# A one-core attention decode kernel: start-up zeroing removed, second V load issued early, tail reordered

## The chip, the cores and the metric

One core of one Trainium2 chip. The metric is the device time of one execution in microseconds, median of several. Executions of the kernel before spread over some 2 us. The span that a profile shows is about 1.8 us shorter than the time (350.1 us and 351.93 us for the profiled execution of before).

A word on two readings that recur. The *timeline* and the *chain of waits* are views of the profile. The *landing* of a load is the time at which the last of its 16 semaphore increments arrived; the trace records it, and tables of landings below are taken from there. The engines have the profile's names: PE is the matmul engine (TensorE), DVE VectorE, ACT ScalarE, POOL GpSimd and SP SyncE, which issues the large loads. The *granted clock* (PEclk) is the share of PE's full clock that the profile records as granted; in the tables it is 1.00 or 0.50, or a mean of the two.

## The reference

A decode step for batch 2: attention of one query over a cache of 4096 keys for 32 heads, a small MLP, and a gate that mixes the two.

```python
# B = 2, Sq = 1, D = 512; H = 32 heads (Hkv = 32 too), Sk = 4096, Dh = 128; Dff = 1376
x = A_x
g = sigmoid((x * gate_w).sum(-1, keepdims=True))
q = x @ A_wq                                  # per head
p = softmax(q k^T * Dh ** -0.5)               # k_cache, v_cache: [B, H, Sk, Dh], bf16
a = (p v) @ A_wo
b = relu(x @ B_w1) @ B_w2
return g * a + (1 - g) * b
```

K and V are 67 MB each and are read once. All inputs together are 145.46 MB.

## The kernel before

Sixteen stages of four heads. In a stage a K tile of 4 MiB is multiplied on the DVE by the query, which has been broadcast over partitions (`mult`), the PE sums the products with an identity matrix (`red_mm`), the DVE finishes the sums, ACT takes the exponential, and the PE multiplies the probabilities with V (`pv`). K and V have two buffers each; every large load is issued by one queue, in order. At the end the heads' outputs are transposed into `OT_sb` and projected with `A_wo` (`wo_mm`), and the result is added (`wo_add`) in the PSUM tile of the MLP's second product (`mlp_o`).

```python
    load(SP, ring("wq"), ...); load(SP, ring("w1"), ...)
    load_k(0); load_k(1); load_v(0)
    ...
    issue(POOL, lambda e: e.memset(vt[1], 0.0), rd=[sel], wr=vb[1])   # the second V buffer
    ...
    # xb[b]: one column of x, broadcast; the queries' matmuls need it
    src = xT.ap[:, :, b : b + 1].to_broadcast([P, DC, TP])
    issue(DVE, ... e.tensor_copy(out=xb[b].ap, in_=src), rd=[xT], wr=[xb[b]])
    ...
    open_loop(NS // 2)          # on PE two stages are one trip of a hardware loop
    for s in range(NS):
        sums_mm(s - 1)
        mult(s, 0); evac(s - 2); expand(s - 1); sums_inv(s - 1)
        red_mm(s, 0); comb_mm(s - 2); mult(s, 1); unpack(s - 2)
        scores(s, 0); red_mm(s, 1); scores(s, 1); probs(s)
        pv(s - 1)               # for s = 0 on the zeroed buffer, result unused
        ...
        load_k(s + 2)           # waits for red_mm(s, 1): the buffer's last reader
        load_v(s + 1)           # waits for pv(s - 1)
        ...                     # at s = NS - 2 the last quarters of A_wo, and B_w2
    close_loop()

    s = NS - 1
    expand(s); evac(s - 1); sums_mm(s); comb_mm(s - 1); unpack(s - 1); sums_inv(s)
    for g in range(NG - 2):                     # half of the projection ...
        for h in range(2):
            wo_mm(g, h)
    pv(s, VC)                                   # ... ahead of the last P.V
    evac(s); comb_mm(s); unpack(s)
    for g in (NG - 2, NG - 1):
        for h in range(2):
            wo_mm(g, h)
    for n in range(len(W2CUTS)):
        if n == 2:
            wo_add()
        mlp_o(n)
    # cast to bf16, store
```

The softmax here doesn't subtract the row's maximum and nothing guards it: scores larger than these inputs give would overflow.

## Time and profile before

| | before |
|---|---|
| time, median of 5 | 352.83 us (351.62 to 353.13) |
| span of the profiled execution | 350.1 us |
| bytes moved | 145.46 MB |
| share of 16 DMA engines' span used by the load queue | 97.2% |
| PE, DVE busy | 60%, 61% |

The page of the kernel before; the two rows of forty entries are equal slices of the span (8.75 us each), the DMA row in tenths:

```profile
span 350.1 us, 2576 instructions
...
DMA  7999999999999999999999999999999999999990
GB/s 307 453 419 427 459 371 427 446 438 421 421 423 453 438 423 419 419 434 420 463 419 423 449 442 423 419 423 457 438 419 419 427 464 424 419 423 427 416 398 14
...
q1 hardware_dynamic: 6628, 145.46, 97.2%
```

DMA is full in every slice but the first and the last. Its rate dips below the usual 416 to 464 in the first slice, the sixth (371) and the last two. So the kernel is a stream of loads, and PE and DVE matter only where they hold the stream up, or where work is left after it.

The landings make this exact (issue and landing in us from the start of the span; "since" is the time since the landing before it):

```
load (KiB)            issue    landing   since
wq   (4096)            0.96     13.31
w1   (1376)            1.41     16.62    3.31
K 1  (4096)            1.88     26.35    9.73
K 2  (4096)            2.35     36.06    9.71
V 1  (4096)            2.92     46.99   10.92   <- 1.2 late
K 3  (4096)           43.93     56.70    9.71
V 2  (4096)           45.78     66.77   10.08   <- 0.4 late
...  every 4096 KiB load 9.71 to 9.74, except
K 15 (4096)          271.12    296.14   10.68   <- 1.0 late
...
w2, last part (128)  328.07    343.76    0.33
```

4 MiB in 9.71 us is 432 GB/s. Everything that lands "late" moves the whole rest of the stream, because the queue is in order (the loads land in the order of their issue) and full (97.2% of the span).

The head on the timeline (start us, duration us, engine, line, operation, output<-inputs, shapes, count; in brackets the idle time before and what ended it):

```profile
4.14 13.75 POOL L451 MEMSET vt<- 128x16384 bf16 x1
...
8.64 9.40 DVE L468 COPY xb<-xT 128x128 bf16<-128x128 bf16 x2
17.96 0.41 DVE L473 COPY gwb<-xT 128x512 bf16<-128x512 bf16 x1
...
29.55 8.72 DVE L594 TENSOR_TENSOR kt<-kt,qb 128x8192 bf16<-128x8192 bf16 x2
...
43.93 0.33 SPq L115 DMA_DIRECT2D kt<-in_A_k_cache_dram  x1
```

POOL fills the second V buffer for 13.75 us. Two small DVE copies beside it take 9.40 us and end 0.15 us after the fill, while a copy four times as large right after takes 0.41. The first K multiply starts 3.2 us after K 1 landed, and K 3 is issued at 43.93, when little is left in the queue.

The tail on the timeline:

```profile
334.12 3.18 PE L270 MATMUL mm<-wbig,OT_sb 128*2 128x512 bf16 x14
...
337.37 2.09 PE L270 MATMUL o<-vt,pt 128*32 128x512 bf16 x26
...
341.45 3.18 PE L270 MATMUL mm<-wbig,OT_sb 128*2 128x512 bf16 x14
...
344.69 1.25 PE L270 MATMUL a<-w,hT 128*2 128x256 bf16 x14
...
346.93 0.42 DVE L809 CAST res<-a 34x256 bf16<-34x256 f32 x1 [1.15 <-PE a L270]
```

The projection (`mm<-wbig,OT_sb`) runs at 0.2 us per matmul, half of it before the last P·V product (`o<-vt,pt`). The chain of waits confirms that the end is PE work (start us, duration us, what):

```profile
337.74 1.77 PE o L270 x23
...
341.52 3.44 PE mm L270 x16
...
346.93 0.42 DVE res L809
```

### The profile page before, as it was taken

The page shows a single profiled execution, that of the slowest core. Times are in us where ns is not written, and L with a number is a line of the kernel's source. Part 1 is how long each engine was busy: PE and PEld are TensorE (multiplying, and loading weights), DVE is VectorE, ACT ScalarE, POOL GpSimd, SP SyncE. Part 2 cuts the span into 40 slices and gives each one's busy share as a digit, 9 for nine tenths or more (in the row PEclk, how much of TensorE's full clock was granted, in tenths as well). Part 3 has the DMA queues.
Part 4 walks back from the last instruction along what each step waited for, and adds up shares of the span by engine and source line. Part 5 has one row for each costly group of instructions (what it writes and reads, how often), then busy time and mean ns, then how long its engine had stood idle before and what let it go on. Part 6 is the DMA issues. An engine that isn't in the chain of part 4 may idle for free.

```text
span 350.1 us, 2576 instructions
## 1 busy us (share of the span) xinstructions
PE 208.7 (60%) x1279; PEld 29.0 (8%) x759; DVE 213.3 (61%) x210; ACT 11.9 (3%) x41; POOL 16.7 (5%) x12
## 2 busy tenths in 40 slices
PE   0082968667629193665709375674928293664966
PEld 0011011010100001010100101010100001010122
DVE  0946495939276583919357492929576582929631
ACT  1022000000000000000000000000000000000000
POOL 8900000000000000000000000000000000000000
PEclk9996789896958678796957879695869878595999
DMA  7999999999999999999999999999999999999990
GB/s 307 453 419 427 459 371 427 446 438 421 421 423 453 438 423 419 419 434 420 463 419 423 449 442 423 419 423 457 438 419 419 427 464 424 419 423 427 416 398 14
DMA packets 6644, 145.53 MB, mean 416 GB/s; under 512 B 743, under 2 KB 878, under 8 KB 1774
## 3 DMA queue, kind: packets, MB, share of 16 engines
q1 hardware_dynamic: 6628, 145.46, 97.2%
q8 instruction: 2, 0.03, 0.0%
q14 instruction: 4, 0.03, 0.0%
q10 hardware_dynamic: 10, 0.00, 0.0%
HBM read 145.46 MB, written 0.00 MB: 415 GB/s over the span
## 4 chain that ended last, share of the span: by engine, by line
DMA 50%; PE 26%; DVE 21%; issue 1%; ACT 1%; ACTq 0%; SPq 0%
DMA kt<-in_A_k_cache_dram 48%; PE red L270 20%; DVE kt L594 15%; PE mm L270 3%; DVE xb L468 3%; DMA x_sb<-in_gate_w_dram 2%; DVE osb L689 2%; PE o L270 1%; PE comb L299 1%; DVE pt L633 1%; PE a L270 1%; ACT h_sb L561 1%; DVE osb L683 0%; PE comb L270 0%; DVE sc L489 0%
## 5 line engine op out<-in xcount | busy, mean ns | idle before, releaser
L270 PE MATMUL red<-kt,ident 128*128 128x512 bf16 x512 | 150.0, 459 | 114.4 <-DVE kt L594 114.4
L594 DVE TENSOR_TENSOR kt<-kt,qb 128x8192 bf16<-128x8192 bf16 x32 | 141.4, 4420 | 56.4 <-DMA kt<-in_A_k_cache_dram 56.4
L489 DVE TENSOR_REDUCE sc<-red 128x64 f32<-128x512 f32 x32 | 22.0, 688 | 47.4 <-PE red L270 47.4
L270 PE MATMUL o<-vt,pt 128*32 128x512 bf16 x544 | 33.1, 380 | 0.0
L269 PEld LDWEIGHTS <-pt 128*32 128x32 bf16 x544 | 13.2, 96 | 66.8 <-issue 55.4
L689 DVE SCALAR_TENSOR_TENSOR osb<-o,jmask,osb 128x128 f32<-128x128 f32 x48 | 16.8, 351 | 1.7
L617 ACT ACTIVATE e<-sc 128x128 bf16<-128x128 f32 x16 | 4.9, 309 | 296.9 <-PE red L270 266.4
L451 POOL MEMSET vt<- 128x16384 bf16 x1 | 13.8, 13752 | 0.1
L269 PEld LDWEIGHTS <-ident 128*128 128x128 bf16 x32 | 3.2, 100 | 119.1 <-DVE kt L594 118.2
L633 DVE TENSOR_TENSOR pt<-e,tmask 128x512 bf16<-128x512 bf16 x16 | 10.9, 682 | 0.5 <-ACT e L617 0.5
L299 PEld LDWEIGHTS comb<-osb,pick 128*64 128x64 f32 x36 | 3.4, 134 | 92.9 <-issue 71.7
L299 PE MATMUL comb<-osb,pick 128*64 128x128 f32 x36 | 7.8, 298 | 3.0 <-DVE osb L689 3.0
L468 DVE COPY xb<-xT 128x128 bf16<-128x128 bf16 x2 | 9.4, 9291 | 0.0
L683 DVE TENSOR_SCALAR osb<-o,jmask 128x128 f32<-128x128 f32 x16 | 5.5, 346 | 5.6 <-PE o L270 5.6
L270 PE MATMUL mm<-wbig,OT_sb 128*2 128x512 bf16 x32 | 7.2, 379 | 0.0
L270 PE MATMUL gs<-xT,gwb 128*128 128x2 bf16 x4 | 0.3, 171 | 10.0 <-DVE gwb L473 10.0
L463 DVE CAST xT<-mm 128x12 bf16<-128x12 f32 x1 | 0.2, 171 | 8.4 <-PE mm L270 8.4
L270 PE MATMUL mm<-ident,x_sb 3*128 3x3 bf16 x4 | 0.3, 173 | 8.1 <-DMA x_sb<-in_gate_w_dram 8.1
L299 PE MATMUL gs<-part,heads 128*64 128x1 f32 x34 | 4.8, 210 | 0.5 <-issue 0.5
L579 DVE CAST hT<-mm 128x22 bf16<-128x22 f32 x1 | 0.2, 181 | 6.7 <-PE mm L270 6.7
L714 DVE SCALAR_TENSOR_TENSOR tmp<-comb,rsg,umask 128x128 f32<-128x128 f32 x8 | 2.8, 349 | 2.1 <-PE comb L299 2.1
L270 PE MATMUL o<-wbig,xb 128*32 128x512 bf16 x32 | 4.0, 483 | 0.0
(54 smaller groups left out, 43.5 us busy)
## 6 DMA issues: line engine op xcount, KB each, us to landing
kt<-in_A_k_cache_dram SPq DMA_DIRECT2D x16, 4096.0 KB, 24.4
vt<-in_A_v_cache_dram SPq DMA_DIRECT2D x15, 4096.0 KB, 32.2
wbig<-in_A_wq_dram SPq DMA_DIRECT2D x1, 4096.0 KB, 12.4
wbig<-in_A_wo_dram SPq DMA_DIRECT2D x2, 1024.0 KB, 31.2
vt<-in_A_v_cache_dram SPq DMA_DIRECT2D x1, 2048.0 KB, 17.4
vt<-in_A_v_cache_dram SPq DMA_DIRECT2D x2, 1024.0 KB, 20.5
wbig<-in_A_wo_dram SPq DMA_DIRECT2D x4, 512.0 KB, 23.5
w<-in_B_w_dram SPq DMA_DIRECT2D x1, 1376.0 KB, 15.2
```

The costliest lines, as they stand in the source:

```text
L269: first = pe.ldweights(lhsT, tile_position=(0, col)) if load_w else None
L270: m = pe.add_instruction(mybir.InstMatmult(name=nc.get_next_instruction_name(), ins=[pe.lower_ap(rhs), pe.lower_ap(lhsT)], outs=[pe.lower_ ...
L299: first = m = nc.tensor.matmul(call[0], lhsT=call[1], rhs=call[2], start=call[3], stop=call[4])
L451: issue(POOL, lambda e: e.memset(vt[1], 0.0), rd=[sel], wr=vb[1])
L468: return e.tensor_copy(out=xb[b].ap, in_=src)
L489: DVE, lambda e: e.reduce_sum(out=dst_ap, in_=src_ap, axis=AX.X), rd=src, wr=dst
L561: return e.activation(out=h_sb.ap[:, cuts[n] : cuts[n + 1]], in_=banks[n].full[:B, : cuts[n + 1] - cuts[n]], func=ACT.Relu, scale=omb.ap,)
L594: DVE, lambda e: e.tensor_tensor(out=k.ap, in0=k.ap, in1=q, op=ALU.mult),
L617: lambda e: e.activation(out=e_sb[n].ap, in_=sc_full[n], func=ACT.Exp, scale=inv_sqrt_dh, accum_out=partials[n].ap,),
L633: DVE, lambda e: e.tensor_tensor(out=dst, in0=e_in, in1=m_in, op=ALU.mult),
L683: DVE, lambda e: e.tensor_scalar_mul(x.ap, view[:, 0, :], jmask.ap[:, 0:1]),
L689: return e.scalar_tensor_tensor(out=x.ap, in0=view[:, j, :], scalar=jmask.ap[:, j : j + 1], in1=x.ap, op0=ALU.mult, op1=ALU.add,)
```

## The change

Its intent: start earlier and with more loads queued, keep instruction fetches of PE away from the stream (in the trace of before a 16 KB instruction packet runs at 42.55 us, for 1.06 us), and shorten what is left after the last load.

```diff
     load_k(0)
     load_k(1)
     load_v(0)
+    load_v(1)
 ...
-    issue(POOL, lambda e: e.memset(vt[1], 0.0), rd=[sel], wr=vb[1])
 ...                       # xb is made 128 wide; the gate's logit by DVE and one matmul
+    issue(DVE, lambda e: e.memset(OT_sb, 0.0), wr=[b for g in OT for b in g])
 ...
+    def emit_pe():         # PE's program: everything up to the loop's end stands in an outer
+        pe.reg_mov(again, 0)        # loop whose first pass jumps over it
+        with pe.Fori(0, 2):
+            with pe.If_ne(again, 0):
+                emit_items(PE.ops[:cut])
+            pe.reg_mov(again, 1)
+        emit_items(PE.ops[cut:])
 ...                       # in the stage loop: P.V and the sums in one block (pv_sums) at the
 ...                       # end; a branch skips P.V in stage 0, so no zeroed buffer is needed
         load_k(s + 2)
-        load_v(s + 1)
+        if s > 0:
+            load_v(s + 1)
 ...
     def wo_mm(g, h):       # the projection in four column groups instead of one
-                (mm.full[:B, :], OT_sb[:, r, :], wo_all[:, r], r == 0, r == NG * DR - 1)
+                (mm.full[r % NCG * CG : (r % NCG + 1) * CG, :], OT_sb[:, r, :], wo_all[:, r],
+                 r < NCG, r >= NG * DR - NCG, r % NCG * CG, ...)
+    def keep_busy(n):      # n matmuls whose result nobody reads
 ...
     evac(s - 1)
-    sums_mm(s)
+    pv_last(s)             # P.V and sums first
     comb_mm(s - 1)
-    unpack(s - 1)
     sums_inv(s)
+    evac(s)
     for g in range(NG - 2): ...wo_mm(g, h)
-    pv(s, VC)
-    evac(s)
+    keep_busy(3)
     comb_mm(s)
     unpack(s)
     for g in (NG - 2, NG - 1):
         for h in range(2):
+            if g == NG - 1:
+                keep_busy(2)
             wo_mm(g, h)
+    keep_busy(5)
```

A switch for loading weights 128 columns wide is in the text of the change but off. Scores, loads' sizes and the stage loop's arithmetic are the same. (Line numbers move: L270, L594 and L115 of before are L286, L630 and L124 after.)

More of the change, by code (lines that the diff above doesn't have):

```diff
@@ L20 @@
 AG = 2
+WIDE = False
 W2CUTS = [0, 5, 8, 10]
@@ L32, with __init__ @@
 class Op:
-    def __init__(self, fn, waits, late=(), inc=None):
+    def __init__(self, fn, waits, late=(), inc=None, skip=False):
         self.fn = fn
+        self.skip = skip
         self.waits = list(waits)
@@ L46, with __init__ @@
 class Engine:
-    def __init__(self, tc, eng, name, rewrites=True):
+    def __init__(self, tc, eng, name, known, rewrites=True):
         self.eng = eng
@@ L52, in __init__ @@
         self.skipped = 0
+        self.known = known
         self.seen = {}
@@ L63, in pending @@
                     need[k] = t
-        for k, t in need.items():
-            self.seen[k] = t[1]
+        implied = [self.known.get((k, t[1]), {}) for k, t in need.items()]
+        for told in implied:
+            need = {k: t for k, t in need.items() if told.get(k, 0) < t[1]}
+        for told in [*implied, {k: t[1] for k, t in need.items()}]:
+            for k, v in told.items():
+                self.seen[k] = max(self.seen.get(k, 0), v)
         return list(need.values())
@@ L79, in step @@
         self.count += n
+        self.known[id(self.sem), self.count] = dict(self.seen)
         return (self.sem, n)
@@ L89, in tokens_of, with done @@
     return out
-def done(engine, token, rd, wr):
+def done(engine, rd, wr):
+    token = (engine.sem, engine.count)
     for b in rd:
@@ L102, in issue @@
     engine.add(Op(fn, need, inc=inc))
-    done(engine, (engine.sem, engine.count), rd, wr)
+    done(engine, rd, wr)
 class Load:
@@ L217 @@
     xT = sb("xT", [P, DC, B + 1], bf16)
-    xb = [sb(f"xb{b}", [P, DC, TP], bf16) for b in range(B)]
-    gwb = sb("gwb", [P, DC, P], bf16)
+    xb = [sb(f"xb{b}", [P, DC, P], bf16) for b in range(B)]
+    zp = sb("zp", [P, B, DC], fp32)
+    zs = sb("zs", [P, B], fp32)
+    ones = sb("ones", [P, P], fp32)
     ge = sb("ge", [P, B], fp32)
@@ L236 @@
     OT = [[Buf() for b in range(B)] for g in range(NG)]
-    OT_sb = mem.tile([P, NG * DR, B], bf16, name="OT_sb")[:]
-    eye = sb("eye", [B, B], fp32)
-    wsum = sb("wsum", [B, D], fp32)
+    OT_sb = mem.tile([P, NG * DR, CG], bf16, name="OT_sb")[:]
+    fold = sb("fold", [P, B], fp32)
+    wsum = sb("wsum", [P, D], fp32)
     res = sb("res", [AR, DG], bf16)
@@ L249 @@
     a_ps = ps("a", AR, DG)
-    PE = Engine(tc, nc.tensor, "pe", rewrites=False)
-    DVE = Engine(tc, nc.vector, "dve")
-    AC = Engine(tc, nc.scalar, "act")
-    POOL = Engine(tc, nc.gpsimd, "pool")
-    SP = Engine(tc, nc.sync, "sp")
+    known = {}
+    PE = Engine(tc, nc.tensor, "pe", known, rewrites=False)
+    DVE = Engine(tc, nc.vector, "dve", known)
+    AC = Engine(tc, nc.scalar, "act", known)
+    POOL = Engine(tc, nc.gpsimd, "pool", known)
+    SP = Engine(tc, nc.sync, "sp", known)
     rings = {}
@@ L264, in size_of, with mm_bf16 @@
         return 32 if n <= 32 else 64 if n <= 64 else 128
-    def mm_bf16(out_, lhsT, rhs, start, stop, col=0, load_w=True):
+    def mm_bf16(out_, lhsT, rhs, start, stop, col=0, weights=True):
         pe = nc.tensor
         ts = (size_of(lhsT.shape[0]), size_of(lhsT.shape[1]))
-        first = pe.ldweights(lhsT, tile_position=(0, col)) if load_w else None
+        first = None
+        if weights is True or (weights is not False and not WIDE):
+            first = pe.ldweights(lhsT, tile_position=(0, col))
+        elif weights is not False:
+            first = pe.ldweights(weights)
         m = pe.add_instruction(
@@ L282, in mm_bf16, with products, emit_calls @@
         return first or m, m
-    def products(calls, wts, rd, wr):
+    def products(calls, wts, rd, wr, skip=False):
         need_w = PE.pending([b.w for b in wts])
         need_m = PE.pending(tokens_of(PE, rd, wr))
-        PE.add(Op(calls, need_w, need_m, PE.step()))
-        done(PE, (PE.sem, PE.count), list(wts) + list(rd), wr)
-    def emit_products(op, need_w, need_m, trip=None):
-        calls = op.fn(trip) if callable(op.fn) else op.fn
-        fused = calls[0][1].dtype == fp32
-        if fused:
+        PE.add(Op(calls, need_w, need_m, PE.step(), skip))
+        done(PE, list(wts) + list(rd), wr)
+    def emit_calls(calls, need_w=(), need_m=()):
+        need_w, need_m = list(need_w), list(need_m)
+        if calls[0][1].dtype == fp32:
             need_w, need_m = [], need_w + need_m
@@ L297, in emit_products @@
         for n, call in enumerate(calls):
-            if fused:
+            if call[1].dtype == fp32:
                 first = m = nc.tensor.matmul(
@@ L308, in emit_products @@
                     m._wait_ge(*need_m[-1])
-        m.then_inc(*op.inc)
+        return m
+    def emit_products(op):
+        emit_calls(op.fn, op.waits, op.late).then_inc(*op.inc)
     def emit_loop(loop):
@@ L313, in emit_loop @@
         first = loop.rounds[0]
-        sites = [[] for _ in first]
-        sems = {}
+        sites = []
         for j in range(len(first)):
-            vals = {}
+            vals, sems = {}, {}
             for k, ops in enumerate(loop.rounds):
@@ L323, in emit_loop @@
                     v[k] = max(v.get(k, 0), val)
+            site = []
             for key, v in vals.items():
@@ L328, in emit_loop @@
                 ks = sorted(v)
-                step = v[ks[1]] - v[ks[0]] if len(ks) > 1 else 0
+                step = v[ks[1]] - v[ks[0]]
                 base = v[ks[-1]] - step * ks[-1]
-                assert ks[-1] == len(loop.rounds) - 1 and ks[0] <= 1 and len(ks) == ks[-1] - ks[0] + 1
-                assert all(v[k] == base + step * k for k in ks)
-                sites[j].append((sems[key], base, step))
-        regs = {}
-        for j, site in enumerate(sites):
-            for n, (sem, base, step) in enumerate(site):
-                if step:
-                    regs[j, n] = pe.alloc_register(f"w{nc.next_id()}")
-                    pe.reg_mov(regs[j, n], base)
@@ L340, in emit_loop @@
-        with pe.Fori(0, len(loop.rounds)) as trip:
-            for j, op in enumerate(first):
-                need = [
-                    (sem, pe.snap(regs[j, n]) if step else base)
-                    for n, (sem, base, step) in enumerate(sites[j])
-                ]
-                for sem, val in need:
-                    pe.wait_ge(sem, val)
-                emit_products(op, [], [], trip)
-            for j, site in enumerate(sites):
-                for n, (sem, base, step) in enumerate(site):
-                    if step:
-                        pe.reg_add(regs[j, n], regs[j, n], step)
+                assert ks[0] <= 1 and ks == list(range(ks[0], len(loop.rounds)))
@@ new lines, in emit_loop @@
+                assert step > 0 and all(v[k] == base + step * k for k in ks)
+                site.append((sems[key], base, step))
+            sites.append(site)
+        order = {}
+        for site in sites:
+            for sem, base, step in site:
+                order.setdefault(step, []).append(base)
+        regs = {step: pe.alloc_register(f"w{nc.next_id()}") for step in order}
+        for step, bases in order.items():
+            pe.reg_mov(regs[step], bases[0])
+        at = {step: 0 for step in order}
@@ new lines, in advance @@
+        def advance(step):
+            bases, n = order[step], at[step]
+            at[step] = n + 1
+            goal = bases[n + 1] if n + 1 < len(bases) else bases[0] + step
+            if goal != bases[n]:
+                pe.reg_add(regs[step], regs[step], goal - bases[n])
+        with pe.Fori(0, len(loop.rounds)) as trip:
+            for op, site in zip(first, sites):
+                need = [(sem, regs[step]) for sem, base, step in site]
+                if op.skip:
+                    assert len(site) == 1 and site[0][1] == 0
+                    with pe.If_ne(need[0][1], 0):
+                        emit_calls(op.fn[:-1], [], need)
+                    emit_calls(op.fn[-1:]).then_inc(*op.inc)
+                else:
+                    emit_calls(op.fn, [], need).then_inc(*op.inc)
+                for sem, base, step in site:
+                    advance(step)
@@ L353, in emit_loop, with emit_items @@
         for r in regs.values():
             pe.free_register(r)
-    def emit_pe():
-        for item in PE.ops:
+    def emit_items(items):
+        for item in items:
             if isinstance(item, Loop):
                 emit_loop(item)
-            elif isinstance(item, Op):
-                emit_products(item, item.waits, item.late)
-            else:
-                item()
+            else:
+                emit_products(item)
+    def emit_pe():
+        pe = nc.tensor
+        cut = 1 + max(n for n, item in enumerate(PE.ops) if isinstance(item, Loop))
+        again = pe.alloc_register("again")
+        pe.reg_mov(again, 0)
[4 more added lines that the diff above has]
+        emit_items(PE.ops[cut:])
@@ L365, in open_loop @@
     def open_loop(trips):
-        loop = Loop(trips)
-        PE.ops.append(loop)
-        PE.loop = loop
+        PE.loop = Loop(trips)
+        PE.ops.append(PE.loop)
     def close_loop():
@@ L466, in spread @@
         def spread(e, b=b):
-            src = xT.ap[:, :, b : b + 1].to_broadcast([P, DC, TP])
+            src = xT.ap[:, :, b : b + 1].to_broadcast([P, DC, P])
             return e.tensor_copy(out=xb[b].ap, in_=src)
         issue(DVE, spread, rd=[xT], wr=[xb[b]])
-    issue(
-        DVE,
-        lambda e: e.tensor_copy(out=gwb.ap, in_=xT.ap[:, :, B:].to_broadcast([P, DC, P])),
-        rd=[xT], wr=[gwb],
-    )
+    fill(DVE, ones, ones.ap, 1.0)
     for n in range(2):
@@ L490, in sum_x @@
         )
-    issue(
-        DVE, lambda e: e.tensor_copy(out=eye.ap, in_=ident.ap[:B, :B]), rd=[ident], wr=[eye]
-    )
+    issue(DVE, lambda e: e.memset(OT_sb, 0.0), wr=[b for g in OT for b in g])
+    sum_x([fold], fold.ap, [ident], ident.ap.rearrange("p (j c) -> p c j", c=CG)[:, :B, :])
     sum_x([umask], umask.ap, [ident], ident.ap.rearrange("p (k a) -> p a k", a=DA))
@@ L499, in gate @@
     def gate():
+        pair = xT.ap[:, :, :B].rearrange("p c b -> p b c")
+        gate_row = xT.ap[:, :, B:].rearrange("p c b -> p b c").to_broadcast([P, B, DC])
+        issue(
+            DVE, lambda e: e.tensor_tensor(out=zp.ap, in0=pair, in1=gate_row, op=ALU.mult),
+            rd=[xT], wr=[zp],
+        )
+        sum_x([zs], zs.ap, [zp], zp.ap)
         z = gs.full[:, :B]
-        products(
-            [(z, gwb.ap[:, c, :], xT.ap[:, c, :B], c == 0, c == DC - 1) for c in range(DC)],
-            [gwb], [xT], [gs],
-        )
+        products([(z, ones.ap, zs.ap, True, True)], [ones], [zs], [gs])
         issue(
@@ L529, in make_qb @@
             [
-                (banks[w].full[t * TP : (t + 1) * TP, :], xb[b].ap[:, c, :], view[:, c, w, t],
-                 c == 0, c == DC - 1, t * TP, w == 0)
+                (banks[w].full[t * TP : (t + 1) * TP, :], xb[b].ap[:, c, t * TP : (t + 1) * TP],
+                 view[:, c, w, t], c == 0, c == DC - 1, t * TP,
+                 (xb[b].ap[:, c, :] if t == 0 else not WIDE) if w == 0 else False)
                 for c in range(DC)
+                for w in range(NW)
                 for t in range(T)
-                for w in range(NW)
             ],
@@ L635, in expand, with sums_call @@
         )
-    def sums_mm(s):
+    def sums_call(s):
         i = s % IG
-        part = partials[s % 2]
-        products(
-            [(gs.ap[CW * i : CW * (i + 1), :], heads.ap, part.ap, True, True)],
-            [heads], [part], [gs],
-        )
+        return (gs.ap[CW * i : CW * (i + 1), :], heads.ap, partials[s % 2].ap, True, True)
     def sums_inv(s):
@@ L658, in sums_inv, with pv_calls, pv_sums, pv_last @@
         )
-    def pv(s, parts=1):
+    def pv_calls(s, q0, q1, wide):
         n, o = s % 2, o_ps[s % 2]
-        per = NQ // parts
-        vs = VC // parts
-        for c in range(parts):
-            products(
-                [
-                    (o.ap[q % NCG * CG : (q % NCG + 1) * CG, :], pt[n].ap[:, q, :],
-                     vt[s % 2][:, q * JB : (q + 1) * JB, :], q < NCG, q >= NQ - NCG,
-                     q % NCG * CG)
-                    for q in range(c * per, (c + 1) * per)
-                ],
-                [pt[n]], vb[s % 2][c * vs : (c + 1) * vs], [o],
-            )
+        return [
+            (o.ap[q % NCG * CG : (q % NCG + 1) * CG, :], pt[n].ap[:, q, :],
+             vt[n][:, q * JB : (q + 1) * JB, :], q < NCG, q >= NQ - NCG, q % NCG * CG,
+             True if not wide else pt[n].ap[:, q : q + NCG, :] if q % NCG == 0 else not WIDE)
+            for q in range(q0, q1)
+        ]
+    def pv_sums(s):
+        n = s % 2
+        calls = pv_calls(s, 0, NQ, True) + [sums_call(s)]
+        if s < 0:
+            products(calls, [heads], [partials[n]], [gs], skip=True)
+        else:
+            products(
+                calls, [pt[n], heads], [*vb[n], partials[n]], [o_ps[n], gs], skip=n == 1
+            )
+    def pv_last(s):
+        n, per = s % 2, NQ // VC
+        for c in range(VC):
+            products(
+                pv_calls(s, c * per, (c + 1) * per, c < VC // 2), [pt[n]], [vb[n][c]], [o_ps[n]]
+            )
+        products([sums_call(s)], [heads], [partials[n]], [gs])
     def evac(s):
@@ L721, in wo_mm @@
     def wo_mm(g, h):
+        r0 = g * DR + h * HR
         products(
             [
-                (mm.full[:B, :], OT_sb[:, r, :], wo_all[:, r], r == 0, r == NG * DR - 1)
-                for r in range(g * DR + h * HR, g * DR + (h + 1) * HR)
+                (mm.full[r % NCG * CG : (r % NCG + 1) * CG, :], OT_sb[:, r, :], wo_all[:, r],
+                 r < NCG, r >= NG * DR - NCG, r % NCG * CG,
+                 OT_sb[:, r : r + NCG, :] if r % NCG == 0 else not WIDE)
+                for r in range(r0, r0 + HR)
             ],
@@ L728, in wo_mm @@
         )
+    def keep_busy(n):
+        products(
+            [(red[0].ap, ident.ap, kb[0][0].ap[:, :, :RW], True, True, 0, k == 0) for k in range(n)],
+            [ident], [kb[0][0]], [red[0]],
+        )
     def wo_add():
-        issue(DVE, lambda e: e.tensor_copy(out=wsum.ap, in_=mm.full[:B, :D]), rd=[mm], wr=[wsum])
+        issue(DVE, lambda e: e.tensor_copy(out=wsum.ap, in_=mm.full[:, :D]), rd=[mm], wr=[wsum])
         products(
             [
-                (a_ps.ap[k * CG : k * CG + B, :], eye.ap, wsum.ap[:, k * DG : (k + 1) * DG],
+                (a_ps.ap[k * CG : k * CG + B, :], fold.ap, wsum.ap[:, k * DG : (k + 1) * DG],
                  False, False)
@@ L737, in wo_add @@
             ],
-            [eye], [wsum], [a_ps],
+            [fold], [wsum], [a_ps],
         )
@@ L760 @@
         PE.loop.at = s // 2
-        sums_mm(s - 1)
         mult(s, 0)
+        sums_inv(s - 2)
         evac(s - 2)
         expand(s - 1)
-        sums_inv(s - 1)
         red_mm(s, 0)
-        comb_mm(s - 2)
         mult(s, 1)
-        unpack(s - 2)
         scores(s, 0)
@@ L773 @@
         probs(s)
-        pv(s - 1)
+        comb_mm(s - 2)
+        pv_sums(s - 1)
+        unpack(s - 2)
         if s % SPG == 2 and s < NS - 2 * SPG:
@@ L816, in store @@
             )
-        engine.add(Op(store, need, inc=(ring(f"out{k}").sem, 16)))
+        engine.add(Op(store, need, inc=(ring("out").sem, 16)))
     with tc.tile_critical(no_gpsimd_drain=True):
@@ L825 @@
         emit_pe()
-        for k in range(AG):
-            nc.sync.wait_ge(ring(f"out{k}").sem, 16)
+        nc.sync.wait_ge(ring("out").sem, 16 * AG)
 _INS = ['A_x', 'A_k_cache', 'A_v_cache', 'A_wq', 'A_wo', 'B_x', 'B_w1', 'B_w2', 'gate_w']
```

## The prediction

> **What bounds the kernel now.** The DMA queue. The page gives the load queue 97.2% of 16 engines' span: 145.46 MB in 350.1 us. In the trace's landing records nearly every 4 MiB load lands 9.71 us after the one before: a constant 432 GB/s. [...] At that rate the bytes need 337 us. Compute per stage (DVE and PE 12 to 13 us of 19.5) is hidden: in the steady loop a K load is issued 24 us before it lands, so some 14 us of loads are still queued. PE and DVE savings inside the loop are worth nothing.
>
> Only three places are not the steady stream:
> - Head: POOL zeroes a V buffer, 13.75 us (4.1 to 17.9). The two DVE copies into xb take 9.4 us, though a copy four times wider beside them takes 0.41; they end when POOL ends [...]. So the first K multiply starts at 29.55, though K landed at 26.35, and the third K load is issued at 43.93, when the queue is nearly empty. Only half the packets are in flight at 45.0, restarting packets take 2 us instead of 1.21, and the first V load lands 1.2 us late. A 16 KB instruction fetch (1.06 us on one DMA engine, at 42.55) falls there too.
> - Rare slips: 0.37 us at 66.8, 0.97 at 296. Kept.
> - Tail: the last load lands at 343.76, but the final cast starts at 346.93, 3.2 us later, because PE is busy with the output projection (32 matmuls, 0.2 us each, serial, half of them before the last P·V). Cast to span end: 3.2 us, kept.
>
> **What the change does.**
> - Removes the POOL memset; the second V buffer is loaded at once. xb copies shrink to about 0.4 us each, the first multiply starts when K lands (26.4), and 53 us of loads are queued at start instead of 44. The hole at 45 us goes: -1.2 us, perhaps -1.5 with the instruction fetch moved to the start by the new outer loop's empty first pass.
> - P·V in one block with the sums, skipped for the first stage: off the path, 0.
> - Tail: the last P·V goes first; the projection uses four column groups. P·V matmuls, already in that form, take 0.06 us each (32 in 1.91 us), so the 32 projections go from 6.4 to about 2 us. Ten keep-busy matmuls add 0.21 us each, partly in idle time. PE should then wait for w2, and the cast start 0.8 us after the last landing, not 3.2: -2.4 us.
>
> Sum: about -4 us: span 346.1, time **348.8 us**, 80% range 346.8 to 350.9. Faster by over 2%: 0.06; within 2%: 0.93; slower by over 2%: 0.01.
>
> **Signs in the profile.** No DMA dip in the slice at 44 to 52 us (371 GB/s now); xb copies under 1 us; first K multiply at 26 to 27; last load landing near 342; the 32 projections in about 2 us; the final cast within 1 us of the last landing; steady loads still 9.71 us apart; PE busy lower, without effect.
>
> **What would make it wrong.** [...] The keep-busy matmuls and projection run behind the loads (tail gain lost). The queue drains at stages 2 or 3, as the third V load now waits for stage 0's product. PE's clock falls in the tail.

The marked cuts take out three passages that no trace of this case shows; the last is a risk put at +8 us. 1.2 to 1.5 us for the head and 2.4 for the tail make the "about -4".

## The result

| | before | after |
|---|---|---|
| time, median | 352.20 us (15 runs, 351.42 to 353.32) | 348.01 us (8 runs, 347.9 to 348.4) |
| span of the profile | 350.1 us | 346.4 us |
| last load lands | 343.76 us | 342.81 us |
| final cast starts | 346.93 us | 343.21 us |
| from last landing to the cast | 3.17 us | 0.40 us |

The ratio is 0.9879, 95% interval 0.9866 to 0.9892. Ratios here are the mean time of one kernel's runs over that of the other's in the same rounds, so not quite the ratio of the medians quoted. By the limit of 2% the two are the same; the 4.2 us between them is nonetheless clear, and it is what the prediction gave (348.8, range 346.8 to 350.9).

The profiles differ by 3.7 us of span: 0.95 us because the loads end earlier, and 2.77 us because less is left after them. The page of the changed kernel:

```profile
span 346.4 us, 2443 instructions
...
DMA  7999999999999999999999999999999999999993
GB/s 301 462 428 424 424 428 435 447 440 422 429 424 424 428 443 439 443 424 407 445 424 428 447 443 435 428 424 424 424 439 439 447 429 424 424 424 431 417 411 131
...
q1 hardware_dynamic: 6628, 145.46, 98.1%
```

The dip in the sixth slice is gone (371 before, 428 now). The landings, though, say something less simple:

```
load (KiB)            issue    landing   since
wq   (4096)            0.94     14.52            <- 1.2 later than before
K 1  (4096)            1.86     27.55    9.71
V 1  (4096)            2.90     46.98    9.71    <- the 1.2 is gone here
V 2  (4096)            3.38     56.69    9.71
K 3  (4096)           41.98     66.42    9.72
...
K 15 (4096)          270.46    295.24   10.13    <- 0.4 late, 1.0 before
...
w2, last part (128)  327.14    342.81    0.32
```

V 1 lands at the same time as before. What was lost at V 1 is now lost at wq. The gain of 0.95 us is nearly all 0.37 at V 2 and 0.55 at K 15, two places that the prediction had marked as "kept".

The head on the timeline, after:

```profile
8.76 0.76 DVE L504 COPY xb<-xT 128x512 bf16<-128x512 bf16 x2
...
27.58 8.76 DVE L630 TENSOR_TENSOR kt<-kt,qb 128x8192 bf16<-128x8192 bf16 x2 [2.18 <-DMA kt<-in_A_k_cache_dram]
...
41.98 0.33 SPq L124 DMA_DIRECT2D kt<-in_A_k_cache_dram  x1
```

The copies take 0.76 us instead of 9.40 although they are four times wider, and the first multiply follows the landing of K 1 (27.55) at once. The idle entry in brackets names that load as what DVE waited for.

The tail on the timeline, after (`red<-kt,ident` are the keep-busy matmuls):

```profile
334.31 0.61 PE L286 MATMUL o<-vt,pt 128*32 128x512 bf16 x8 [1.09 <-DMA vt<-in_A_v_cache_dram]
...
335.23 1.05 PE L286 MATMUL mm<-wbig,OT_sb 128*32 128x512 bf16 x16
...
337.38 0.62 PE L286 MATMUL mm<-wbig,OT_sb 128*32 128x512 bf16 x8
...
338.46 0.40 PE L286 MATMUL mm<-wbig,OT_sb 128*32 128x512 bf16 x4
...
339.41 0.40 PE L286 MATMUL mm<-wbig,OT_sb 128*32 128x512 bf16 x4
...
339.74 1.25 PE L286 MATMUL red<-kt,ident 128*128 128x512 bf16 x5
...
341.92 0.49 PE L286 MATMUL a<-w,hT 128*2 128x256 bf16 x6 [0.19 <-DMA w<-in_B_w_dram]
...
343.21 0.42 DVE L864 CAST res<-a 34x256 bf16<-34x256 f32 x1 [2.67 <-PE a L286]
```

The last eight matmuls of P·V now wait for their V chunk, sixteen projections take 1.05 us (3.18 for fourteen before), and the last products wait for `w2`. The chain of waits now ends in a load, with 1.3 us of PE's work behind it (this load is the second part of `w2`, landed at 341.88; the last part lands at 342.81, while PE is still at that work):

```profile
317.71 24.17 DMA w<-in_B_w_dram
...
341.92 0.49 PE a L286 x6
...
343.21 0.42 DVE res L864
```

### The profile page after: what moved, and what is told of

Read it like the earlier page. It is cut to its first block, busy times and chain, and to the rows that moved or that the text cites. A ratio compares the mean times of both kernels' runs of the same rounds, so it can differ in the third digit from the quotient of the medians.

```text
span 346.4 us, 2443 instructions
## 1 busy us (share of the span) xinstructions
PE 203.8 (59%) x1257; PEld 27.0 (8%) x729; DVE 204.9 (59%) x213; ACT 11.9 (3%) x41; POOL 3.0 (1%) x11
## 4 chain that ended last, share of the span: by engine, by line
DMA 62%; DVE 21%; PE 13%; SPq 2%; issue 1%; DVEq 0%
DMA kt<-in_A_k_cache_dram 55%; DVE kt L630 18%; PE red L286 12%; DMA w<-in_B_w_dram 7%; DVE osb L733 2%; SPq L124 2%; DVE pt L669 1%; PE o L286 1%; DVE osb L727 0%; PE a L286 0%; PE comb L314 0%; PE a L314 0%; DVE res L864 0%; PE gs L314 0%; SPq L907 0%
## 5 line engine op out<-in xcount | busy, mean ns | idle before, releaser
L286 PE MATMUL red<-kt,ident 128*128 128x512 bf16 x524 | 151.7, 454 | 122.2 <-DVE kt L630 122.2
L630 DVE TENSOR_TENSOR kt<-kt,qb 128x8192 bf16<-128x8192 bf16 x32 | 141.4, 4421 | 57.5 <-DMA kt<-in_A_k_cache_dram 57.5
L286 PE MATMUL o<-vt,pt 128*32 128x512 bf16 x512 | 30.7, 380 | 1.1 <-DMA vt<-in_A_v_cache_dram 1.1
L283 PEld LDWEIGHTS <-pt 128*32 128x32 bf16 x512 | 12.2, 96 | 14.3 <-issue 4.0
L669 DVE TENSOR_TENSOR pt<-e,tmask 128x512 bf16<-128x512 bf16 x16 | 10.9, 681 | 0.0
L286 PE MATMUL mm<-ident,x_sb 3*128 3x3 bf16 x4 | 0.3, 173 | 8.2 <-DMA x_sb<-in_gate_w_dram 8.2
L286 PE MATMUL o<-wbig,xb 128*32 128x512 bf16 x32 | 4.0, 474 | 0.0
L314 PEld LDWEIGHTS gs<-part,heads 128*64 128x64 f32 x34 | 3.2, 134 | 6.8 <-issue 6.8
L653 ACT ACTIVATION_READ_ACCUMULATOR e<-sc 128x1 f32 x16 | 3.0, 186 | 0.0
L286 PE MATMUL mm<-wbig,xb 128*32 128x512 bf16 x16 | 2.5, 592 | 0.4 <-DMA wbig<-in_A_wq_dram 0.4
```

Source lines behind the costliest of these rows:

```text
L283: first = pe.ldweights(lhsT, tile_position=(0, col))
L286: m = pe.add_instruction(mybir.InstMatmult(name=nc.get_next_instruction_name(), ins=[pe.lower_ap(rhs), pe.lower_ap(lhsT)], outs=[pe.lower_ ...
L314: first = m = nc.tensor.matmul(call[0], lhsT=call[1], rhs=call[2], start=call[3], stop=call[4])
L630: DVE, lambda e: e.tensor_tensor(out=k.ap, in0=k.ap, in1=q, op=ALU.mult),
L653: lambda e: e.activation(out=e_sb[n].ap, in_=sc_full[n], func=ACT.Exp, scale=inv_sqrt_dh, accum_out=partials[n].ap,),
L669: DVE, lambda e: e.tensor_tensor(out=dst, in0=e_in, in1=m_in, op=ALU.mult),
```

## The experiments

Where an edit is given against the changed kernel or against the one before, nothing else differs. Each job of four kernels had its own runs of the kernel before: medians 353.01 (e1 to e4), 351.85 (e5 to e8) and 352.63 us (e9 to e12), 11 runs each. All twelve results were correct.

### e1 and e9: the tail alone

```diff
 # the kernel before, with of the change only: OT_sb 32 wide and zeroed by DVE, wo_mm in four
 # column groups, fold instead of eye, keep_busy, and
+    pv(s, VC)
     sums_mm(s)
     comb_mm(s - 1)
     sums_inv(s)
+    evac(s)
     for g in range(NG - 2): ...
+    keep_busy(3) ...
```

> The kernel before with the tail of the changed kernel and nothing else. In the traces the final cast starts 3.17 us after the last landing before and 0.40 us after the change, so if the tail pays by itself it gives 2.8 us: 349.4 to 349.8 us, with the head's landings (wq at 13.3, first V at about 47.0) as before. If the last landing moved because the tail also changed the loads, it lands clearly earlier than 343.8.

> e1 once more, on the same chip and in the same rounds as e10, because the kernel before varied by over 1 us between e1's session and e6's. Third K load issued at 44 to 45, that load or the V load ahead of it late by 1 to 2 us in all. 349.2 to 349.8; if e6's 348.1 was only a better session, this falls to 348.1 too.

Measured: 349.49 us, ratio 0.9913 (0.9891 to 0.9935), and again 349.60 us, ratio 0.9921 (0.9898 to 0.9944). The last landing is at 344.28 and 344.15, no earlier than before, and the store is issued 0.80 us after it. The tail alone is worth about 3 us of the 4.2. The landings also show a cost: K 3 is issued at 44.90 and 44.74 instead of 43.93, and then K 3 itself lands late. The zeroing of `OT_sb`, which is new on DVE in the head, is not on the path: DVE is done by 22.8 and in e1 then idles 6.8 us for PE. The queries' matmuls start at 18.6 as before, but the granted clock rises to full only at 23.03 and 22.83, not at 21.73 (in before and e9 groups of four matmuls start every 0.43 us until then and every 0.21 us after), so they end later and the first K multiply starts at 30.18 and 30.08 instead of 29.55. Whether the edit shifted the clock or it varies from execution to execution, no run shows.

### e2: the head alone

```diff
 # the changed kernel, with the tail of before: projection serial, half of it ahead of pv_last,
 # no keep_busy
```

> The changed kernel with the tail of the kernel before (projection ahead of the last P.V, serial, no keep-busy). Theory A (prediction: the hole after the first loads was a drained queue, the head pays 1.2 to 1.5 us): 350.7 to 351.0. Theory B (the 1.2 us was the 16 KB instruction fetch taking one packet's place on one DMA engine, and the change only moved it to 5.4 us): the head pays about 0.4 to 0.9, by smaller slips alone, 351.3 to 351.8.

Measured: 352.22 us, ratio 1.000 (0.9974 to 1.0026): above the ranges of both theories, so it doesn't decide between them. Two of the six runs lay at 353.7 and 354.2. The last landing is 343.03, 0.7 us earlier than before, but the store is issued at 347.67, 0.3 us later: with the old tail the end hangs on a chain of compute from the last K load, not on the last landing. My rebuilt tail isn't quite that of before either: the sums of the last stage come after P·V, so that the chain from the last K landing to the cast is 1.0 us longer. What it does show: an earlier last landing gains nothing while PE is what ends last.

### e3: where the 1.2 us at V 1 came from

```diff
 # the changed kernel
     def emit_pe():
-        ...                # outer loop with an empty first pass
+        emit_items(PE.ops)
```

> The changed kernel without the outer loop's empty first pass; the queue cannot drain here (53 us queued at the start). Theory A (drain): the landing of wq goes back to 13.3, nothing is lost later, the last landing comes 1.2 us earlier and the time falls to about 346.8. Theory B (fetch): the 16 KB fetch is again in the middle, near 41 us, and costs its 1.2 us there; wq lands at 13.3, some load near 42 to 47 lands 1.2 late, total unchanged at 348.0 within 0.3.

Measured: 348.03 us (348.01 to 348.11), the same as the changed kernel. wq lands at 13.40, V 1 at 10.72 after the load before it. In the trace the 16 KB instruction packet starts at 39.99 instead of 5.36. The queue was far from empty (the loads up to 56 us were queued from the start), so no drain can explain the late V 1. This settles it for theory B. The packets of one DMA engine in the changed kernel show how it happens (my grouping of packets into engines, by which packet starts as another ends; start-end in us, size, queue):

```
2.09-4.10(32K q1) 4.10-5.33(32K q1) 5.37-6.29(16K q8) 6.31-7.53(32K q1) 7.52-8.74(32K q1)
```

A 32 KB packet of a load takes 1.21 us; the instruction packet (queue 8) takes 0.92 us in its place, and a load is only landed when its slowest engine is done: of the 16 increments of wq, fifteen are in by 13.15 us and the last comes at 14.52; of those of V 1 in the kernel before, fifteen by 45.78 and the last at 46.99. Over all fourteen profiles it holds for this first 16 KB fetch: in the eight with the fetch at 5.2 to 5.5 us, wq lands at 14.3 to 14.7; in the other six (fetch at 38.8 to 46.5) at 13.2 to 13.5, and V 1 is 1.0 to 1.3 us late in the five of them in which the fetch came at 43.54 or earlier. It does not hold for the second one, which every profile has at 335.6 to 343.2 us (1.10 to 1.11 us long): the 512 KiB load in whose stretch it falls lands 1.26 to 1.30 us after the one before, like its neighbours.

### e4: memset and late V load put back

```diff
 # the changed kernel
-    load_v(1)
+    issue(POOL, lambda e: e.memset(vt[1], 0.0), rd=[sel], wr=vb[1])
 ...
-        if s > 0:
-            load_v(s + 1)
+        load_v(s + 1)
```

> The changed kernel with the POOL memset and the late second V load put back; the empty first pass stays. First K multiply at about 29.5 again. Theory A: the queue drains near 45 us and 1 to 1.2 us are lost again, 349.2. Theory B: the fetch at the start has pushed the stream 1.2 us back, the third K load comes in time, total 348.0 to 348.4.

Measured: 354.13 us, ratio 1.0035: 6 us slower than the changed kernel, and outside what both theories expected. The reason is in the timeline: the change computes the gate's logit on DVE, behind all the fills, and PE's in-order program cannot start on the queries before it. With DVE held up until 18.5 us, PE starts on the queries at 23.07 (18.62 in the kernel before), the first K multiply starts at 35.39, not at 29.5, and K 3 is issued at 48.31. K 3 then lands 13.44 us after the load before it, 3.7 late. As a test of the memset alone it is spoiled; as a view of a truly drained queue it is useful, and it led to e10.

### e5: the early V load

```diff
 # the changed kernel
-    load_v(1)
 ...
-        if s > 0:
-            load_v(s + 1)
+        load_v(s + 1)
```

> The changed kernel with only the second V load put back to stage 0 (the memset stays away). The queued loads end near 46 us, 1.2 us later than before because of the fetch at the start; the third K load is issued near 42. If only an actual drain costs, nothing drains and the time is 348.0 within 0.3. If the early V load itself is what pays, the time rises by 0.5 to 1.5 us.

Measured: 347.97 us (347.83 to 348.10). The early second V load is worth nothing by itself; K 3, issued at 41.52, lands 9.72 after the load before it.

### e6: the memset off POOL

```diff
 # e1's kernel
-    issue(POOL, lambda e: e.memset(vt[1], 0.0), rd=[sel], wr=vb[1])
 ...
     gate()
+    issue(DVE, lambda e: e.memset(vt[1], 0.0), wr=vb[1])
```

> The kernel before with the new tail (e1, 349.5) and, of the head, only the memset moved from POOL to DVE, after the gate. DVE is then free at 8.4 us, the first K multiply starts at about 26.4 instead of 29.55, the third K load is issued near 41 instead of 44 to 45, before the queue is empty at 45. If the head's gain is only that the queue no longer drains there, this gives the whole gain: 348.0 to 348.3, with the later slips near 67 and 287 to 296 us falling to about 0 and 0.4 us. If the early V load or the empty first pass is needed, it stays at 349 or above.

Measured: 348.13 us (347.91 to 348.43), ratio 0.9889 (0.9871 to 0.9907): the whole gain of the change, without its early V load, its skipped P·V and its empty first pass. The head on e6's timeline:

```profile
8.71 0.36 DVE L467 COPY xb<-xT 128x128 bf16<-128x128 bf16 x2
...
15.49 6.88 DVE L761 MEMSET vt<- 128x8192 uint32 x1 [1.65 <-issue]
...
26.23 8.76 DVE L592 TENSOR_TENSOR kt<-kt,qb 128x8192 bf16<-128x8192 bf16 x2 [1.28 <-DMA kt<-in_A_k_cache_dram]
...
40.33 0.33 SPq L115 DMA_DIRECT2D kt<-in_A_k_cache_dram  x1
```

and that of e9, the same kernel with the memset on POOL:

```profile
4.13 13.75 POOL L451 MEMSET vt<- 128x16384 bf16 x1
...
8.71 9.31 DVE L468 COPY xb<-xT 128x128 bf16<-128x128 bf16 x2
...
30.08 8.72 DVE L593 TENSOR_TENSOR kt<-kt,qb 128x8192 bf16<-128x8192 bf16 x2
...
44.74 0.33 SPq L115 DMA_DIRECT2D kt<-in_A_k_cache_dram  x1
```

The two copies into xb take 0.36 us instead of 9.31. DVE fills the same buffer in 6.88 us at a time when it has nothing else to do, the first multiply follows K 1's landing, and K 3 is issued 4.4 us earlier. K 3 lands 9.70 after the load before it, V 2 on time as well; a V load issued at 253.07 is 0.8 late, so e6 does not gain all that the changed kernel gained late in the stream. e6 and e9 did not run in the same rounds, but each had a variant of the changed kernel beside it: e6 is 0.16 us slower than e5 (347.97), e9 1.56 us slower than e12 (348.04). So the difference between e6 and e9 is not one of sessions.

### e10: how much delay the queue can take

```diff
 # e6's kernel, before the stage loop
+    for c in (slice(0, NC), slice(0, NC // 4)):
+        issue(DVE, lambda e, c=c: e.memset(vt[1][:, c], 0.0), wr=vb[1])
     open_loop(NS // 2)
```

> e6 (348.1) with 8.6 us more of DVE memsets before the first K multiply, of which about 7 us delay it: third K load issued at about 47.5 instead of 40.3. Drain theory: data in the queue end at 45.6 on fifteen engines, the restart begins at about 48.6 with slow first packets, that K load lands at about 59.2 instead of 56.5, the later slips show in full (1.4 us together instead of 0.4 to 0.8), time 351 to 351.8. If compute delay at the head is absorbed by the 14 us of slack of the steady stream, time stays at 348.1.

Measured: 355.32 us (353.7 to 356.45), ratio 1.0071. The delay came out larger than planned, since the extra fills waited too:

```profile
36.55 8.69 DVE L592 TENSOR_TENSOR kt<-kt,qb 128x8192 bf16<-128x8192 bf16 x2
...
51.27 0.33 SPq L115 DMA_DIRECT2D kt<-in_A_k_cache_dram  x1
```

The multiply starts 10.3 us later than in e6 and K 3 is issued 10.9 us later, but lands only 6.9 us later (63.47 and 56.55). The first 4 us were free. In the four profiles with K 3 issued at 44.7 or later, it landed 12.1 to 12.3 us after its issue. So in these profiles K 3 lands at the later of two times: the landing before plus 9.71, or its issue plus 12.2. By that, an estimate, in e6, with a landing due at 56.55, the issue may be as late as 44.35 (56.55 - 12.2); in the kernel before, with one due at 56.70, as late as 44.50. That kernel, at 43.93 in its profile, stood 0.6 us from its edge; e1 and e9 were over it and their K 3 was 0.75 and 0.23 us late.

The late landings, all of them over the usual 9.71 us, put side by side:

```
                 K 3 issued   K 3 late   V 2 late   later (253-271 us issue)   time (median)
before              43.93        0         0.4            1.0                   352.2
e9 (tail only)      44.74        0.2       0.6            1.0                   349.6
e1 (tail only)      44.90        0.75      0.4            1.0                   349.5
e4                  48.31        3.7       0.6            1.0                   354.1
e10                 51.27        7.8       0.55           1.0                   355.3
e6                  40.33        0         0              0.8                   348.1
after               41.98        0         0              0.4                   348.0
e2, e3, e5, e7, e8,
e11, e12           40.9-42       0         0              0.2-0.7               -
```

Where the queue came near its end or past it, two later loads are late by more than otherwise. Why, no run shows.

The traces do tie these later slips to instruction fetches as well. In each of the fourteen profiles two 8 KB instruction packets (queue 14, 0.31 to 0.33 us long) run in mid-stream, the first at 54.9 to 71.9 us, the second at 284.3 to 291.9. Every late V 2 of the table has the first packet between the landing before it and its own, and every later late load has the second packet there (in e5 the packet starts 0.01 us too early for that). In the nine other profiles the first packet falls to a load that lands on time. So a fetch is met with at each slip, but not a slip at each fetch; why not was not shown.

### e7: without the keep-busy matmuls

```diff
 # the changed kernel
-    keep_busy(3)
 ...
-            if g == NG - 1:
-                keep_busy(2)
 ...
-    keep_busy(5)
```

> The changed kernel without the ten keep-busy matmuls. If the tail waits for the last landing, and the granted clock stays full anyhow, the time stays at 348.0 within 0.2. If they hold the clock up, the granted clock falls to half in the last 10 us and the tail gets 0.3 to 0.6 us longer.

Measured: 349.14 us (348.90 to 349.35), 1.1 us slower than the changed kernel, about twice what was expected. Stretches of 2 us in the changed kernel, with busy time of each engine, granted PE clock, DMA share and rate:

```profile
core 0: us, PE busy (x) PEld busy (x) DVE busy (x) ACT busy (x) POOL busy (x), PEclk, DMA share, GB/s
338.00:340.00 2.00, 1.99 (x14) 0.49 (x11) 0.31 (x2) 0.00 (x0) 0.00 (x0) 1.00 0.97 378
340.00:342.00 2.00, 1.78 (x17) 0.59 (x14) 0.55 (x1) 0.00 (x0) 0.00 (x0) 1.00 0.33 123
342.00:344.00 2.00, 1.17 (x16) 0.67 (x14) 0.42 (x1) 0.00 (x0) 0.00 (x0) 1.00 0.01 4
```

and in e7:

```profile
338.00:340.00 2.00, 0.80 (x8) 0.21 (x9) 0.32 (x1) 0.00 (x0) 0.00 (x0) 1.00 0.98 380
340.00:342.00 2.00, 1.15 (x12) 0.79 (x13) 0.37 (x1) 0.00 (x0) 0.00 (x0) 0.50 0.30 111
342.00:344.00 2.00, 1.89 (x18) 0.74 (x14) 0.07 (x1) 0.00 (x0) 0.00 (x0) 0.65 0.01 2
```

Without the fillers PE is busy for 0.80 us of the 2 us up to 340, and its granted clock is 0.50 from 340.00 to 342.00 and 0.65 in the mean of the next 2 us, just when the last products run. They take longer (sixteen products with `w2` 1.87 us in e7, the same in two parts 0.71 and 0.49 in the changed kernel; the four of `wo_add` 1.05 against 0.60), and the cast starts at 343.93 although the last load landed at 342.66: 1.27 us after, against 0.40.

### e8: projection serial

```diff
 # the changed kernel
-                (mm.full[r % NCG * CG : ..., :], OT_sb[:, r, :], wo_all[:, r], r < NCG, ...)
+                (mm.full[:B, :], OT_sb[:, r, :B], wo_all[:, r], r == 0, r == NG * DR - 1)
```

> The changed kernel with the projection in one column group (serial, 0.2 us each) but still after the last P.V. 32 matmuls take 6.4 instead of about 2 us; with the keep-busy matmuls in the same in-order engine PE runs behind the loads: final cast 2 to 3 us after where it is now, 350 to 351.

Measured: 352.81 us, 4.8 us slower than the changed kernel; I had expected 2 to 3. The projection on e8's timeline:

```profile
335.32 3.61 PE L286 MATMUL mm<-wbig,OT_sb 128*2 128x512 bf16 x16
...
339.98 1.89 PE L286 MATMUL mm<-wbig,OT_sb 128*2 128x512 bf16 x8
...
348.00 0.42 DVE L862 CAST res<-a 34x256 bf16<-34x256 f32 x1 [2.43 <-PE a L286]
```

Sixteen projections take 3.61 us, the next eight 1.89 and the last two fours 1.02 each, where the column groups took 1.05, 0.62 and 0.40 twice. That is 5.1 us more, nearly all of it on PE's in-order path, since the keep-busy matmuls, no longer idle filler, stand in the same path. (The edit also narrows `wo_add` to the 2 rows that this form fills, as before the change.) The size of the loss is that of this combination, not what column groups would give the kernel before.

### e11: half of the projection ahead of P·V again

```diff
 # the changed kernel
-    pv_last(s)
     comb_mm(s - 1)
-    sums_inv(s)
-    evac(s)
     for g in range(NG - 2): ...wo_mm(g, h)
+    pv_last(s)
+    sums_inv(s)
+    evac(s)
```

> The changed kernel with the first half of the projection (four column groups, about 1 us) put back ahead of the last P.V. P.V ends about 2.5 us later (337 instead of 334.9), evacuation and the rest of the chain follow it; the final cast about 1 us later: 348.6 to 349.2. If the loads still hide it, 348.0.

Measured: 349.23 us (349.13 to 349.45), 1.2 us slower. The order on e11's timeline:

```profile
333.64 1.05 PE L286 MATMUL mm<-wbig,OT_sb 128*32 128x512 bf16 x16
...
334.51 1.90 PE L286 MATMUL o<-vt,pt 128*32 128x512 bf16 x32
...
344.17 0.42 DVE L864 CAST res<-a 34x256 bf16<-34x256 f32 x1 [2.21 <-PE a L286]
```

P·V now ends at 336.4, not at 334.9, and the cast starts at 344.17 with the last landing at 342.69. So each of the three parts of the tail (order, column groups, keep-busy) is needed; they don't add up, since each is measured with the other two in place.

### e12: an attempt to beat both

```diff
 # the changed kernel
-        if n == 2:
+        if n == 1:
             wo_add()
```

> An attempt to beat both: the changed kernel with the projection's add before the second w2 block, not after it, into PE's wait for the loads. PE then has 0.5 us less to do after the last landing but one; at best 0.1 to 0.2 us, 347.8 to 348.0, within noise.

Measured: 348.04 us, the same. With 0.40 us between last landing and cast there is little left to take.

## Why the prediction was right

The total was right: 348.01 us against 348.8, the span 346.4 against 346.1. Its parts were less right than the sum, and that the sum fits is partly luck: the head was put 0.25 us or more too high and the tail 0.37 too low, and the head's gain came by another path than the one predicted. Two of the signs were off with it: the first K multiply starts at 27.58, not at 26 to 27, and the last load lands at 342.81, not near 342.

- **The bound** was right. Every profile shows 9.71 us per 4 MiB while the queue is full, and PE's busy time fell by 5 us while the loads stayed 9.71 us apart.
- **The tail** was right in mechanism and a little too small: predicted 2.4 us, 2.77 in the profiles, about 3 in e1 and e9. The term that was mis-sized is the time from last landing to cast: 0.8 predicted, 0.40 measured.
- **The keep-busy matmuls** had been entered as a cost of 0.21 us each. e7 shows them to be worth 1.1 us; the risk "PE's clock falls in the tail" would have come true without them (a granted clock of 0.50 in e7, 1.00 in the changed kernel, from 340 to 342 us).
- **The head** was predicted at 1.2 to 1.5 us, and its profile gave 0.95, for partly other reasons. The step that failed is "The hole at 45 us goes: -1.2 us". The 1.2 us of the first V load was the 16 KB instruction fetch, not the emptying queue: e3 has a full queue and the late V load. The step "perhaps -1.5 with the instruction fetch moved to the start" failed too: at the start the stream is already full at 5.4 us, and the fetch costs its packet's place there (wq at 14.52 instead of 13.31).
- **"Rare slips ... Kept"** was wrong as well. They are where the head's gain lies: 0.37 and 0.55 us, each at a load in whose stretch an 8 KB instruction packet runs.
- **The memset's hold on the DVE copies** was right (9.31 us beside the POOL memset in e9, 0.36 in e6), and it is the part of the head that matters: e6 reaches 348.1 with nothing else from the head. The danger it had caused was real, but it lay 0.6 us away in the profile of before and was only met in e1 and e9, which have the same memset and a later rise of the clock. Why executions of before vary by 2 us and those of the changed kernel by 0.5 stays open: the edge would explain it, but e2, whose K 3 is issued at 41.4 and is nowhere near it, varied by 2.2 us too, and no profile of a slower execution was taken.
- **The early V load and the empty first pass** are worth nothing here (e5, e3).

## What to carry to other kernels

In a stream that is full, list the landings and look for those that come late; each is an event to look into, and here only these and the time after the last landing could be gained. Moving a disturbance to another place in a full stream need not remove it (the 16 KB fetch cost wq the 1.2 us that it had cost V 1), so count it at its new place too. In a tail that waits for loads, look at the granted clock and try matmuls that fill the waits (without them it was 0.50 here, and the time 1.1 us longer), put the longest dependent chain first, and check with one experiment per part, since a total can come out right with its parts wrong.
